# Attention and MLP block on one core: bias loaded by rows and turned on TensorE, first tiles of x from two queues, one tile's statistics on ScalarE

## The chip, the cores and the metric

The kernel runs on one NeuronCore of a Trainium2 chip. The metric is device time in microseconds (us); several executions were timed and the median stands for the kernel. One further execution was taken with the hardware profiler; its trace is read below.

The core's engines run side by side, each with a stream of instructions of its own, executed in order: TensorE (PE: matmuls, and transposes as matmuls with an identity), VectorE (DVE), ScalarE (ACT), GpSimd (POOL) and SyncE (SP), which here only issues DMAs. An engine that needs another's result waits on a semaphore, and whatever stands behind the waiting instruction on its engine waits too. SBUF is the on-chip memory (128 partitions), PSUM the accumulator that TensorE writes.

## The reference

x is 1 x 2048 x 512 in float32. A layer norm feeds attention with 32 query heads of 16 that share one key and value head; the normed x feeds both branches, x itself only the last sum:

```python
x = A_x
xn = _layernorm(x, axis=-1)              # (x - mean) / sqrt(var + 1e-5) over 512
s = _A_ref(xn, A_wq, A_wk, A_wv, A_wo)   # softmax(q k^T / 4) v, then @ wo
g = _silu(_B_ref(xn, B_w1, B_b1, B_w2))  # mish(xn @ w1 + b1) @ w2, 1792 wide
return x + s * g
```

So every product starts from the row statistics of x, and `b1` is added to the first MLP product, feature by feature.

## The kernel before

x is taken in 16 tiles of 128 rows, four to a block; block 0 is tiles 0 to 3. The program has a lead of some 75 us, in which the blocks are normed, turned and projected to keys and values and the first scores are made, and then a steady part, in which TensorE goes through scores, row maxima, value products and the MLP's products.

Numbers in float32 are multiplied as two parts: `hi` (rounded to the matmul format) and `lo` (the rest), so weights and x pass through a split (`split`, L460; for the key and value weights `wk_split`, L384) before a matmul reads them.

The start, by engine:

- **SP** issues the loads in the order in which the Python code calls them: `load_x(0)` (L381 calls L221 to L231: tiles 0 to 3 of x), the first query weights (`rawwq`, L514), then `load_x(1)`, in which tile 4 is followed by the two small loads `wkv` of the key and value weights (L229, L230), and further tiles, the first MLP weights, `b1` (L1292) and the other tiles.
- **POOL** clears some tiles (L195 to L199) and then runs `wk_split` (L384 to L389): four times a copy to the high part, a plain copy and a subtraction, twelve instructions on 128 x 64. They are recorded when `load_x(1)` is called, so they stand early in POOL's stream. Behind them stand the low parts of the first query weights (`wq`) and MLP weights (`xtw`).
- **DVE** takes the statistics of each tile (`stats`, L237: `bn_stats` and `bn_aggr` into `mvs`, mean and variance per row). After four tiles `norm_a` (L257) makes variance plus epsilon for the four at once (`ve`), ACT takes its power -1/2 with Ln and Exp (`norm_b`, L260), DVE refines it and makes `nbias` (`norm_c`, L264).
- Then `x_scale` (L284) norms the tiles, tiles 0 and 2 on DVE (L287) and 1 and 3 on ACT (L211); PE turns them (`x_transpose`, L293), ACT and DVE take them out as `xt` (L307, L169), and PE makes the first queries (`xps`, L112) and keys and values (`kp`, L339).
- For tiles 12 to 15 the statistics are on ACT (`stats_sum`, `stats_var`, L242 to L249), in two passes of 512 with accumulation.
- PE runs 24 matmuls on cleared data at the start (`warm`, L1299), and single ones later (L1384), whose results nobody reads.

The order inside each engine's stream in the lead comes from a small planner (L1286 to L1506): it holds tasks with guessed durations, dependencies and arrival times (`xat`), steps through its own clock, always takes the task that can start first, and records it there. It knows nothing of instructions that are recorded outside it, such as `wk_split`. A task is a Python function: if it has instructions for several engines, all are recorded at that moment.

`b1c` is `b1` as 14 columns of 128 partitions. It is loaded by one DMA in which each element is its own 4-byte piece, and its first reader is the bias addition at L785, in the MLP. `v_transpose` and `v_out` (L363, L374) turn the values of a block into `vaug`; for block 0 the copy out is on DVE.

Of the kernel before, what the change touches and what calls it, by code (L numbers as in the profile page):

```python
# [14 lines left out]
F32 = mybir.dt.float32  # L15
F32R = mybir.dt.float32r
AF = mybir.ActivationFunctionType
ALU = mybir.AluOpType
AX = mybir.AxisListType

P = 128
S = 2048
D = 512
# [7 lines left out]
NFT = F // P  # L31
# [91 lines left out]
def block_kernel(ctx: ExitStack, tc: tile.TileContext, x, wq, wk, wv, wo, w1, b1, w2, out):  # L123
    nc = tc.nc
    cp = ctx.enter_context(tc.tile_pool(name="const", bufs=1))
    sb = ctx.enter_context(tc.tile_pool(name="work", bufs=2))
    ps_e = ctx.enter_context(tc.tile_pool(name="ps_e", bufs=3, space=bass.MemoryType.PSUM))
    ps_m = ctx.enter_context(tc.tile_pool(name="ps_m", bufs=3, space=bass.MemoryType.PSUM))
    ps_v = ctx.enter_context(tc.tile_pool(name="ps_v", bufs=1, space=bass.MemoryType.PSUM))
# [4 lines left out]
    pe, act, dve, pool, sp = nc.tensor, nc.scalar, nc.vector, nc.gpsimd, nc.sync  # L134
# [51 lines left out]
    ident = cp.tile([P, P], F32, name="ident")  # L186
# [15 lines left out]
    b1c = cp.tile([P, NFT], F32, name="b1c")  # L202
# [4 lines left out]
    xr = x.rearrange("o (t p) d -> (o t) p d", p=P)  # L207
# [7 lines left out]
    def new_xt(c):  # L215
        xt_of[c] = sb.tile([P, 2, NDT, C], F32R, tag="xt", name=f"xt{c}", bufs=2)
        return xt_of[c]

    xin = {}

    def load_x(c):  # L221
        for tt in range(4):
            if 4 * c + tt < NPT:
                xin[c, tt] = pts[:, 4 * c + tt]
            else:
                xin[c, tt] = sb.tile([P, D], F32, tag=("y0", "sc")[tt % 2], name=f"xin{c}_{tt}", bufs=1)
            sp.dma_start(xin[c, tt], xr[4 * c + tt])
            if (c, tt) == (1, 0):
                sp.dma_start(wkv[:, 0], wk.rearrange("(t p) n -> p t n", p=P))  # L229
                sp.dma_start(wkv[:, 1], wv.rearrange("(t p) n -> p t n", p=P))  # L230
                wk_split()  # L231

    mvs = cp.tile([P, NKT, 2], F32, name="mvs")

    nms = cp.tile([P, 4], F32, name="nms")

    def stats(t):  # L237
        st = sb.tile([P, 6], F32, tag="st", name=f"st{t}")
        dve.bn_stats(st, xin[divmod(t, 4)])
        dve.bn_aggr(mvs[:, t], st)  # L240

    def stats_sum(t):  # L242
        w = sb.tile([P, D], F32, tag="u", name=f"sq{t}", bufs=2)
        act.activation(w, xin[divmod(t, 4)], AF.Identity, scale=-1.0 / 8192, accum_out=nms[:, t - 12:t - 11])

    def stats_var(t):
        w = sb.tile([P, D], F32, tag="t", name=f"sv{t}", bufs=2)
        act.activation(w, xin[divmod(t, 4)], AF.Square, scale=1.0 / 16, bias=nms[:, t - 12:t - 11],
                       accum_out=mvs[:, t, 1:2])  # L249
# [74 lines left out]
    vp_of = {}  # L324
# [38 lines left out]

    def v_transpose(c):
        if c == 0:
            vp = vp_of[c] = ps_v.tile([P, 4, 32], F32, tag="v", name=f"vp{c}")
            for tt in range(4):
                pe.transpose(vp[:, tt], vt_of[c][0:32, P * tt:P * (tt + 1)], ident[0:32, 0:32])
        else:
            vp = vp_of[c] = ps_v.tile([P, 2, 2, HALF], F32, tag="v", name=f"vp{c}")  # L370
            for j in range(2):
                pe.transpose(vp[:, j], vt_of[c][:, P * j:P * (j + 1)], ident)

    def v_out(c):  # L374
        if c == 0:
            dve.tensor_copy(vaug[:, 0:4, 0:DH], vp_of[c][:, :, 16:32])
        else:
            act.activation(vaug[:, 4 * c:4 * c + 4, 0:DH].rearrange("p (h j) n -> p h j n", h=2),
                           vp_of[c][:, :, :, 48:64].rearrange("p j h n -> p h j n"), AF.Copy)

    load_x(0)  # L381
    wkv = sb.tile([P, C], F32, tag="xr", name="wkv", bufs=4)
    wkv = wkv[:, 0:2 * NDT * DH].rearrange("p (a t n) -> p a t n", a=2, t=NDT)
    def wk_split():  # L384
        for j in range(4):
            o = slice(DH * j, DH * (j + 1))
            hi_pool(wk3[:, 0, :, o], wkv[:, j // 3])
            pool.tensor_copy(wkf[:, :, o], wkv[:, j // 3])
            sub(pool, wk3[:, 1, :, o], wkv[:, j // 3], f(wk3[:, 0, :, o]))  # L389
# [55 lines left out]
    def arrived(tag):  # L445
        k, n = todo[tag]
        if taken(tag, k) or tag == "ws" and k < 12 and k > posted[0] + (4 if lead and now[0] < 50 else 2):
            return False
        return k < n and items[tag][k].step + 1 <= (step[0] if lead else max(step[0], step_of(busy[0])) + 0.3)
# [45 lines left out]
    def load(tag):  # L495
        its = items[tag]
        k, n = todo[tag]
        if tag == "wx" and m1_done.get((NC - 2, NFT - 1)) is None or lead and tag == "wq" and n > 1:
            return
        if n == len(its):  # L500
            return
        it = its[n]
        if taken(tag, n) and (tag != "ws" or kept.get(it.key)):
            return
        if n == k and kept.get(it.key):
            it.tile = home(tag, n)
            sp.dma_start(f(it.tile), kept[it.key])
            it.ready = math.ceil(2 * (sp_at(0.5) + 1.6)) / 2
            todo[tag][:] = n + 1, n + 1
        elif n - k < NRAW[tag] and freed and freed[0] <= step[0] + (0.1 if lead else 0.8):  # L510
            freed.popleft()
            r = sb.tile([P, D], F32, tag="raw", name=f"raw{tag}{n}", bufs=RAWS)
            if len(it.src.shape) == 3:
                sp.dma_start(r.rearrange("p (t n) -> p t n", t=NDT), it.src)  # L514
            else:
                sp.dma_start(r, it.src)
            it.raw, it.step = r, (lead["arrive"]() if lead else sp_at(0.45))
            todo[tag][1] += 1
# [712 lines left out]
    plan = {e: [] for e in T}  # L1231
# [19 lines left out]
    def task(eng, us, fn, deps=(), **kw):  # L1251
        t = Task(eng, us, fn, deps, **kw)
        plan[eng].append(t)
        return t
# [28 lines left out]

    step[0] = (0.0 - E0) / STEP_US
    new_xt("w")
    xat = {0: 3.4, 1: 3.8, 2: 4.6, 3: 5.3}  # L1286
    dma_t[0], T["SP"] = 6.4, 2.0
    load("wq")
    load_x(1)
    xat.update({t: landed(DMA_US) for t in range(4, 8)})  # L1290
    load("ws")
    sp.dma_start(b1c, b1.rearrange("(t p) -> p t", p=P))  # L1292
    load_x(2)
    load_x(3)
    xat.update({t: landed(DMA_US) for t in range(8, 16)})
# [7 lines left out]
    def bank(tag, n, t, users):  # L1303
# [3 lines left out]
        b.append([t, *users])  # L1307

    st = [task("DVE", 0.83, lambda t=t: stats(t), at=xat[t], prio=t // 4 * 2) for t in range(12)]
    for t in range(12, 16):  # L1310
        ss = task("ACT", 0.8, lambda t=t: stats_sum(t), at=xat[t], prio=4)
        st.append(task("ACT", 0.8, lambda t=t: stats_var(t), [ss], prio=4))
    kv_done = None
    for c in range(NC):
# [56 lines left out]
        if c == 0:  # L1371
            vc.deps = [kl]
        bank("v", 1, k0, [kh, vc] if 0 < c < 3 else [kl, vc])
        vtr = task("PE", 0.5, lambda c=c: v_transpose(c), [vc], fill=c > 0)
        vo = task("ACT" if c else "DVE", 0.24, lambda c=c: v_out(c), [vtr])
        bank("v", 1, vtr, [vo])

# [42 lines left out]
    def soon(k, t):  # L1420

        return all(d.end is not None and d.end < t + 2.0 or d.end is None and d.deps and d.eng != "DVE" and all(x.end is not None for x in d.deps)
                   for d in k.deps)
# [4 lines left out]
    while True:  # L1428
# [59 lines left out]
        elif k == "J":  # L1488
            tag = next((g for g in ("wq", "ws", "wb") if not any(soon(k, s) for k in plan["POOL"]) and arrived(g) and busy[0] + E0 < s + (4.5 if g == "ws" else 0.5)), None)
            n = ran[0]  # L1490
# [193 lines left out]
```

## Time and profile before

| | |
|---|---|
| median of 3 executions | 1570.08 us (1569.93 to 1570.16) |
| the profiled execution | 1572.05 us |
| its span, first to last instruction | 1570.3 us |
| mean granted clock of TensorE in it | 0.997 |
| instructions in the span | 31407 |

The span is what the trace shows; the profiled execution's own time is 1.75 us longer, and 1.97 us longer than the median. The views used here are the page's share of busy time, the chain of waits that ended last (followed back from the last instruction to the first), the timeline of an engine, and the table of windows, which gives for chosen stretches the busy time of engines, the granted clock of TensorE, the busy share of the 16 DMA engines and the rate. A DVE or ACT instruction on a full tile of 128 x 512 float32 takes some 0.5 to 0.8 us here, so a few microseconds of the lead are a handful of instructions.

### The profile page before, as it was taken

What the parts mean: (1) busy time and instruction counts of PE and PEld (TensorE: products, weight loads), DVE (VectorE), ACT (ScalarE), POOL (GpSimd) and SP (SyncE); (2) the same over time, 40 slices, a digit from 0 to 9 for tenths busy, and PEclk for the clock granted to TensorE, in tenths of its full rate; (3) what the DMA queues carried; (4) which work ended last, traced back from release to release, by engine and by line L of the source; (5) the groups of instructions that cost most, each with busy time, mean ns of one, the idle gap of its engine ahead of it and who ended that gap; (6) DMA issues with size and microseconds to landing.
All of it is one profiled execution on the core that took longest, in us unless ns stands there. A gap on an engine that the chain in (4) does not pass through costs nothing.

```text
span 1570.3 us, 31407 instructions
## 1 busy us (share of the span) xinstructions
PE 1556.2 (99%) x11723; PEld 879.3 (56%) x11723; DVE 1348.8 (86%) x2281; ACT 1289.8 (82%) x2501; POOL 635.7 (40%) x668
## 2 busy tenths in 40 slices
PE   9999999999999999999999999999999999999998
PEld 5555655655555565565555556556555555655654
DVE  7998888888988988888998988888889998888844
ACT  5588888789898778977989788897788978888786
POOL 4687448356357202431624422163152323315022
PEclk9999999999999999999999999999999999999999
DMA  6233134133151303203113320322321213031110
GB/s 199 95 128 129 39 103 139 44 112 112 36 162 52 104 21 112 72 19 104 52 51 116 92 92 17 103 67 80 101 59 49 91 57 117 16 98 32 47 49 28
DMA packets 73863, 125.47 MB, mean 80 GB/s; under 512 B 21536, under 2 KB 35136, under 8 KB 73712
## 3 DMA queue, kind: packets, MB, share of 16 engines
q1 hardware_dynamic: 73568, 123.21, 25.3%
q8 instruction: 93, 1.52, 0.4%
q14 instruction: 58, 0.48, 0.1%
q10 hardware_dynamic: 144, 0.26, 0.0%
HBM read 75.57 MB, written 26.21 MB: 65 GB/s over the span
## 4 chain that ended last, share of the span: by engine, by line
PE 95%; ACT 2%; DVE 1%; DMA 1%; issue 0%; POOL 0%; SPq 0%; DVEq 0%; POOLq 0%; ACTq 0%
PE xps L116 43%; PE pv L1131 32%; PE m L1073 12%; PE e L1044 6%; PE xps L112 1%; ACT pts L1049 1%; DVE mb L1077 1%; PE kp L339 0%; DMA pts<-in_dram 0%; PE xp L298 0%; PE wop L116 0%; DMA rawwb<-in_dram 0%; PE warm L1384 0%; PE wop L112 0%; ACT xt L307 0%
## 5 line engine op out<-in xcount | busy, mean ns | idle before, releaser
L1077 DVE TENSOR_REDUCE mb<-m 128x1 f32<-128x512 f32 x2048 | 1266.8, 684 | 170.9 <-PE m L1073 145.4
L1049 ACT ACTIVATE pts<-e 128x512 f32<-128x512 f32 x2038 | 1060.1, 607 | 221.0 <-PE e L1044 152.3
L1073 PE MATMUL m<-ks,qt 48*128 48x512 f32 (+1 forms) x2048 | 842.5, 425 | 0.7 <-DVE mb L1077 0.5
L1044 PE MATMUL e<-qt,ks 64*128 64x512 f32 x2048 | 750.2, 407 | 2.1 <-ACT pts L1049 1.9
L1131 PE MATMUL pv<-pts,vaug 128*32 128x512 f32 x4076 | 530.1, 603 | 0.0
L1073 PEld LDWEIGHTS m<-ks,qt 48*128 48x128 f32 (+1 forms) x2048 | 368.1, 185 | 105.8 <-DVE mb L1077 53.4
L1044 PEld LDWEIGHTS e<-qt,ks 64*128 64x128 f32 x2048 | 373.9, 186 | 26.4 <-ACT pts L1049 12.6
L116 PE MATMUL xps<-wbs,act 64*128 64x512 f32 x1248 | 315.3, 397 | 0.0
L116 PE MATMUL xps<-xt,ws 64*128 64x512 f32 x1128 | 313.0, 410 | 0.4 <-ACT pts L1049 0.3
L116 PEld LDWEIGHTS xps<-xt,ws 64*128 64x128 f32 x1128 | 194.3, 185 | 183.0 <-ACT pts L1049 121.4
L116 PEld LDWEIGHTS xps<-wbs,act 64*128 64x128 f32 x1248 | 226.2, 185 | 65.3 <-ACT pts L1049 32.7
L1131 PEld LDWEIGHTS pv<-pts,vaug 128*32 128x32 f32 x4076 | 88.1, 108 | 151.4 <-issue 143.5
L169 POOL TENSOR_TENSOR hb<-hb,t 128x512 f32<-128x512 f32 x56 | 72.2, 1289 | 167.9 <-ACT t L804 87.7
L179 POOL TENSOR_SCALAR t<-t 128x512 f32<-128x512 f32 x56 | 34.4, 615 | 174.7 <-ACT t L791 174.6
L116 PE MATMUL xps<-xt,wq 64*128 64x512 f32 x336 | 93.1, 410 | 0.0
L116 PEld LDWEIGHTS xps<-xt,wq 64*128 64x128 f32 x336 | 57.9, 185 | 54.8 <-ACT pts L1049 37.7
L169 POOL TENSOR_TENSOR oc<-oc,sc 128x512 f32<-128x512 f32 (+1 forms) x16 | 20.7, 1291 | 153.7 <-DMA qt<-qh 78.6
L116 PE MATMUL xps<-wbs,ot_all 64*128 64x512 f32 x288 | 79.3, 408 | 0.0
L116 PEld LDWEIGHTS xps<-wbs,ot_all 64*128 64x128 f32 x288 | 49.5, 184 | 46.7 <-ACT pts L1049 28.5
L169 POOL TENSOR_TENSOR act<-hb,act 128x512 fp32r<-128x512 f32 x56 | 72.1, 1288 | 4.7
L169 POOL TENSOR_TENSOR hb<-hb,u 128x512 f32<-128x512 f32 x56 | 72.2, 1289 | 4.4
L169 POOL TENSOR_TENSOR u<-u,t 128x512 f32<-128x512 f32 x56 | 71.9, 1285 | 4.7
(154 smaller groups left out, 898.1 us busy)
## 6 DMA issues: line engine op xcount, KB each, us to landing
wbs<-w SPq DMA_DIRECT2D x38, 512.0 KB
ws<-w SPq DMA_DIRECT2D x36, 512.0 KB
qt<-qh SPq DMA_DIRECT2D x256, 32.0 KB
w<-wbs SPq DMA_DIRECT2D x14, 512.0 KB
wq<-wq SPq DMA_DIRECT2D x14, 512.0 KB
wbs<-wo SPq DMA_DIRECT2D x12, 512.0 KB
rawws<-in_dram SPq DMA_DIRECT2D x20, 256.0 KB
w<-ws SPq DMA_DIRECT2D x10, 512.0 KB
```

The source lines that it names most:

```text
L112: self.pe.matmul(ps, self.lhs(), self.rhs(), start=(self.k == 0), stop=(self.k == self.tot - 1))
L116: i = self.pe.matmul(ps, self.lhs()[o], self.rhs()[o], start=(self.k == 0 and self.halves == 0), stop=(self.k == self.tot - 1 and self.hal ...
L169: eng.tensor_tensor(out=o, in0=a, in1=b, op=op)
L179: pool.tensor_scalar(o, o, lim, 0.0, op0=ALU.min, op1=ALU.max)
L1044: pe.matmul(e, ks[o:o + 64, P * k:P * (k + 1)], q[o:o + 64, p], start=True, stop=True)
L1049: x = act.activation(dst, e, AF.Exp, scale=0.25)
L1073: pe.matmul(m, q[o, p, P * t:P * (t + 1)], ks[o, C * kb:C * (kb + 1)], start=True, stop=True)
L1077: return dve.reduce_max(out=mb_of[v][:, kb, z:z + 1], in_=m, axis=AX.X)
L1131: pe.matmul(o[32 * j:32 * j + 32], vaug[:, k], pt, start=(k == 0), stop=(k == 15))
```

## The change

Three things are done in one edit.

1. Tiles 1 and 3 of x are issued from ACT's queue, tiles 0 and 2 from SP's as before.
2. The statistics of tile 1 go from DVE (`stats(1)`) to a new task `stats_one` on ACT: a pass with Identity that sums -x/8192, a pass with Square around that sum, and then two POOL instructions that scale the sums into `mvs` for tile 1. DVE keeps tiles 0, 2 and 3.
3. `b1` is loaded as 14 rows of 128 (`b1r`), turned by one PE transpose into the PSUM tile in which block 0's values are turned, and copied to `b1c` by ACT.

```diff
--- before.py
+++ after.py
@@ -224,13 +224,14 @@
                 xin[c, tt] = pts[:, 4 * c + tt]
             else:
                 xin[c, tt] = sb.tile([P, D], F32, tag=("y0", "sc")[tt % 2], name=f"xin{c}_{tt}", bufs=1)
-            sp.dma_start(xin[c, tt], xr[4 * c + tt])
+            (act if c == 0 and tt % 2 else sp).dma_start(xin[c, tt], xr[4 * c + tt])
             if (c, tt) == (1, 0):
                 sp.dma_start(wkv[:, 0], wk.rearrange("(t p) n -> p t n", p=P))
                 sp.dma_start(wkv[:, 1], wv.rearrange("(t p) n -> p t n", p=P))
                 wk_split()
 
     mvs = cp.tile([P, NKT, 2], F32, name="mvs")
+    b1r = cp.tile([NFT, P], F32, name="b1r")
 
     nms = cp.tile([P, 4], F32, name="nms")
 
@@ -238,6 +239,16 @@
         st = sb.tile([P, 6], F32, tag="st", name=f"st{t}")
         dve.bn_stats(st, xin[divmod(t, 4)])
         dve.bn_aggr(mvs[:, t], st)
+
+    ms1 = cp.tile([P, 2], F32, name="ms1")
+
+    def stats_one():
+        x_ = xin[0, 1]
+        w = [sb.tile([P, D], F32, tag=g, name=f"s1{g}", bufs=2) for g in "ut"]
+        act.activation(w[0], x_, AF.Identity, scale=-1.0 / 8192, accum_out=ms1[:, 0:1])
+        act.activation(w[1], x_, AF.Square, scale=1.0 / 16, bias=ms1[:, 0:1], accum_out=ms1[:, 1:2])
+        pool.tensor_scalar(mvs[:, 1, 0:1], ms1[:, 0:1], -16.0, 0.0, op0=ALU.mult, op1=ALU.add)
+        pool.tensor_scalar(mvs[:, 1, 1:2], ms1[:, 1:2], 0.5, 0.0, op0=ALU.mult, op1=ALU.add)
 
     def stats_sum(t):
         w = sb.tile([P, D], F32, tag="u", name=f"sq{t}", bufs=2)
@@ -363,7 +374,10 @@
 
     def v_transpose(c):
         if c == 0:
-            vp = vp_of[c] = ps_v.tile([P, 4, 32], F32, tag="v", name=f"vp{c}")
+            v_b1 = ps_v.tile([P, P + NFT], F32, tag="v", name=f"vp{c}")
+            vp = vp_of[c] = v_b1[:, 0:P].rearrange("p (t n) -> p t n", n=32)
+            vp_of["b1"] = v_b1[:, P:P + NFT]
+            pe.transpose(vp_of["b1"], b1r, ident[0:NFT, 0:NFT])
             for tt in range(4):
                 pe.transpose(vp[:, tt], vt_of[c][0:32, P * tt:P * (tt + 1)], ident[0:32, 0:32])
         else:
@@ -374,6 +388,7 @@
     def v_out(c):
         if c == 0:
             dve.tensor_copy(vaug[:, 0:4, 0:DH], vp_of[c][:, :, 16:32])
+            act.activation(b1c, vp_of["b1"], AF.Copy)
         else:
             act.activation(vaug[:, 4 * c:4 * c + 4, 0:DH].rearrange("p (h j) n -> p h j n", h=2),
                            vp_of[c][:, :, :, 48:64].rearrange("p j h n -> p h j n"), AF.Copy)
@@ -1283,13 +1298,13 @@
 
     step[0] = (0.0 - E0) / STEP_US
     new_xt("w")
-    xat = {0: 3.4, 1: 3.8, 2: 4.6, 3: 5.3}
+    xat = {0: 4.3, 1: 4.3, 2: 4.6, 3: 5.3}
     dma_t[0], T["SP"] = 6.4, 2.0
     load("wq")
     load_x(1)
     xat.update({t: landed(DMA_US) for t in range(4, 8)})
     load("ws")
-    sp.dma_start(b1c, b1.rearrange("(t p) -> p t", p=P))
+    sp.dma_start(b1r, b1.rearrange("(t p) -> t p", p=P))
     load_x(2)
     load_x(3)
     xat.update({t: landed(DMA_US) for t in range(8, 16)})
@@ -1307,6 +1322,8 @@
         b.append([t, *users])
 
     st = [task("DVE", 0.83, lambda t=t: stats(t), at=xat[t], prio=t // 4 * 2) for t in range(12)]
+    plan["DVE"].remove(st[1])
+    st[1] = task("ACT", 1.7, stats_one, at=xat[1], lat=0.5)
     for t in range(12, 16):
         ss = task("ACT", 0.8, lambda t=t: stats_sum(t), at=xat[t], prio=4)
         st.append(task("ACT", 0.8, lambda t=t: stats_var(t), [ss], prio=4))
```

What stands now in each engine's stream, where it matters. On POOL, at the end of `wk_split` (`wk` and `wkf` are its outputs, `mvs` the statistics, `wq` and `xtw` the low parts of weights). Before:

```order
L164 TENSOR_SCALAR wk_90<-wkv 128x4x16 [waits DMAHW7_49]
L388 COPY wkf<-wkv 128x4x16
L169 TENSOR_TENSOR wk_90<-wkv,wk_90 128x4x16 [waits Pool_49]
L169 TENSOR_TENSOR wq_193<-rawwq_115,wq_193 128x512 [waits DMAHW4_49,Activation_49]
L169 TENSOR_TENSOR xtw<-rawws_135,xtw 128x512 [waits DMAHW3_49,Activation_49]
```

and now (line numbers are those of the changed file):

```order
L164 TENSOR_SCALAR wk_90<-wkv 128x4x16 [waits DMAHW7_49]
L403 COPY wkf<-wkv 128x4x16
L169 TENSOR_TENSOR wk_90<-wkv,wk_90 128x4x16 [waits Pool_49]
L250 TENSOR_SCALAR mvs<-ms_107 128x1 [waits Activation_49]
L251 TENSOR_SCALAR mvs<-ms_107 128x1 [waits Activation_49]
L169 TENSOR_TENSOR wq_198<-rawwq_117,wq_198 128x512 [waits DMAHW4_49,Activation_49]
L169 TENSOR_TENSOR xtw<-rawws_137,xtw 128x512 [waits DMAHW3_49,Activation_49]
```

The two instructions that finish tile 1's statistics came in behind all twelve instructions of `wk_split`.

On DVE, from the statistics to `ve` (`norm_a`). Before:

```order
L239 BN_STATS st_180<-pts 128x6 [waits DMAHW2_49]
L240 BN_AGGR mvs<-st_180 128x2 [waits DVE_49]
L239 BN_STATS st_183<-pts 128x6 [waits DMAHW3_49]
L240 BN_AGGR mvs<-st_183 128x2 [waits DVE_49]
L258 TENSOR_SCALAR ve<-mvs 128x4 [waits DVE_49]
```

and now:

```order
L240 BN_STATS st_185<-pts 128x6 [waits DMAHW3_49]
L241 BN_AGGR mvs<-st_185 128x2 [waits DVE_49]
L240 BN_STATS st_188<-pts 128x6 [waits DMAHW2_49]
L241 BN_AGGR mvs<-st_188 128x2 [waits DVE_49]
L269 TENSOR_SCALAR ve<-mvs 128x4 [waits DVE_49,Pool_49]
```

`ve` of block 0 waited for DVE alone and now waits for POOL as well.

On ACT, after the power for block 2 (`rstd`), where the bias is copied out (`vp` is the shared PSUM tile, `sq` and `sv` the statistics of tile 12, `xf` the turned tile 7). Before:

```order
L262 ACTIVATE rstd<-rstd 128x4 [waits Activation_49]
L244 ACTIVATE sq_373,nms<-pts 128x512 [waits DMAHW1_49]
L248 ACTIVATE sv_390,mvs<-pts,nms 128x512 [waits Activation_49]
L316 ACTIVATE xf_0_329<-xp_385 128x2x128 [waits PE_49]
L316 ACTIVATE xf_1_330<-xp_385 128x2x128
```

and now:

```order
L273 ACTIVATE rstd<-rstd 128x4 [waits Activation_49]
L391 ACTIVATE b1c<-vp_362 128x14 [waits DVE_49,PE_49]
L255 ACTIVATE sq_380,nms<-pts 128x512 [waits DMAHW1_49]
L259 ACTIVATE sv_397,mvs<-pts,nms 128x512 [waits Activation_49]
L327 ACTIVATE xf_0_334<-xp_392 128x2x128 [waits PE_49]
L327 ACTIVATE xf_1_335<-xp_392 128x2x128
```

The copy of the bias came in ahead of the statistics, with a wait for DVE: the DVE instruction that it waits for is the copy of block 0's values out of the same PSUM tile. Beside these rows only the matching ones changed: two DMA issues and two activations at the head of ACT's stream, one pair of statistics gone from DVE's, one transpose more on PE. All other instructions stand in the order in which they stood.

## The prediction

> **What bounds the kernel now.** The page's busy shares come first:
>
> ```profile
> PE 1556.2 (99%) x11723; PEld 879.3 (56%) x11723; DVE 1348.8 (86%) x2281; ACT 1289.8 (82%) x2501; POOL 635.7 (40%) x668
> ```
>
> TensorE works all the time, and none of its real work is touched. What the change can move is how late the steady part begins, so the start of the chain of waits is next (start, length, what):
>
> ```profile
> 1.64 4.70 DMA pts<-in_dram
> ...
> 7.89 0.19 DVE mvs L240
> ...
> 8.11 0.18 DVE ve L258
> ...
> 9.62 1.53 ACT pts L211 x2
> ...
> 11.17 2.07 ACT xt L307 x4
> ...
> 13.29 3.20 PE xps L112 x12
> ...
> 16.51 0.60 ACT qh L723
> 17.11 0.12 ACT rstd L261
> ...
> 19.32 0.78 POOL pts L287
> ...
> 20.14 0.66 PE xp L298 x4
> ```
>
> The reader is to see that `ve` at 8.11 us is the neck: norming, turning, first queries, block 1's norm follow from it one after the other, and in each engine's stream all other work stands behind it. Only loads and POOL's `wk_split` run without it. What makes `ve` late by some time makes the lead late by as much; I see no slack behind it, since what is loaded later waits for buffers that this chain frees.
>
> **Part 1: POOL.** The timeline of POOL (start, length, engine, line, what):
>
> ```profile
> 3.46 1.84 POOL L199 MEMSET qt<- 128x1024 f32 x2
> 9.33 0.24 POOL L164 TENSOR_SCALAR wk<-wkv 128x64 fp32r<-128x64 f32 x1 [4.03 <-DMA wkv<-in_dram]
> ...
> 10.01 0.42 POOL L164 TENSOR_SCALAR wk<-wkv 128x64 fp32r<-128x64 f32 x1
> ...
> 11.13 0.23 POOL L164 TENSOR_SCALAR wk<-wkv 128x64 fp32r<-128x64 f32 x1
> ...
> 12.46 1.29 POOL L169 TENSOR_TENSOR wq<-rawwq,wq 128x512 fp32r<-128x512 f32 x1
> ...
> 18.18 0.20 POOL L275 TENSOR_SCALAR hv<-hv 128x4 f32<-128x4 f32 x1
> 18.45 0.20 POOL L276 TENSOR_TENSOR rstd<-hv,rstd 128x4 f32<-128x4 f32 x1
> ```
>
> POOL is idle for 4.03 us until `wkv` lands at 9.33, then splits until 12.46, and the two instructions that finish tile 1's statistics stand behind that. `ve` waits for them. Before, `ve` was done before the split began. Three of the four rounds of the split take 0.67 us (9.33 to 10.01, and two from 11.13 to 12.46) and one, in which DVE normed tiles, 1.12 (10.01 to 11.13). In the changed kernel DVE stands still meanwhile, so I take 4 x 0.67 = 2.7 us; at most it is the 3.13 of before. The two small instructions cost one step of 0.27 and 0.20 (18.18, 18.45), and 0.05 for the semaphore.
>
> When does `wkv` land? SP's queue issues tiles 0 to 3 in
>
> ```profile
> 0.74 1.81 SPq L227 DMA_DIRECT2D pts<-in_dram  x4
> ```
>
> and the windows show how busy the DMA engines then are (length, busy us and count of PE, PEld, DVE, ACT, POOL, then clock, DMA share, GB/s):
>
> ```profile
> 2.00:3.00 1.00, 1.00 (x2) 0.81 (x3) 0.00 (x0) 0.01 (x1) 1.00 (x2) 1.00 0.80 287
> 3.00:4.00 1.00, 1.00 (x4) 0.80 (x3) 0.53 (x1) 0.00 (x0) 1.00 (x3) 1.00 0.89 307
> 4.00:5.00 1.00, 1.00 (x4) 0.81 (x3) 0.93 (x4) 0.00 (x0) 1.00 (x2) 1.00 0.88 250
> ```
>
> The same bytes stand ahead of `wkv` as before. Two issues of 0.45 us leave SP's queue, but the DMA engines are 80 to 89% busy from 2 us on, so there is 0.20 + 0.11 + 0.12 = 0.4 us to win. I take 0.2, between 0 and 0.5. [...]
>
> So `ve` starts at 9.33 - 0.2 + 2.7 + 0.52 = 12.35, which is **4.2 us late**; bounds 9.33 - 0.5 + 2.7 + 0.52 - 8.11 = 3.9 and 9.33 + 3.13 + 0.52 - 8.11 = 4.9. I take 4.3, because POOL's low part of `wq`, which ran after DVE's norming, now falls into it, and that norming may lose some tenths (the round of 1.12 shows that the two disturb each other).
>
> The gains of the change are hidden by this: DVE has one tile less to take and tiles may land sooner, but DVE then waits for POOL until 12.3. ACT's two passes cost what those of tile 12 cost:
>
> ```profile
> 23.85 0.61 ACT L244 ACTIVATE sq<-pts 128x512 f32<-128x512 f32 x1
> ...
> 25.22 0.19 ACT L248 ACTIVATION_READ_ACCUMULATOR sv<-pts,nms 128x1 f32 x1
> 25.24 0.22 DVE L376 COPY vaug<-vp 128x64 f32<-128x64 f32 x1
> ...
> 25.58 0.66 ACT L316 ACTIVATE xf<-xp 128x256 f32<-128x256 f32 x2 [0.17 <-PE xp L298]
> ...
> 28.53 1.98 PE L339 MATMUL kp<-xf,wkf 128*64 128x256 f32 x8
> ```
>
> 25.22 + 0.19 - 23.85 = 1.6 us, from about 4 to 6 us, before POOL can use them. Cost nothing; without the split ahead on POOL they would end before tile 3's statistics.
>
> **Part 2: the bias.** The load by rows replaces one of 4-byte pieces in SP's queue; nobody waited for that. The transpose adds at most the 0.16 us of one of four in `20.14 0.66`, in a stretch where PE waits for loads. ACT's copy waits for DVE's copy of `vaug`, which stands behind four maxima on DVE. In the times of before that holds ACT from 23.9 to 25.46; behind it are the statistics of tile 12 (1.6 us) and `xf`, which would be done at 25.5 + 0.25 + 1.6 + 0.66 = 28.0 instead of 26.24. The reader of that `xf` is `kp` at 28.53. So it is hidden with 0.5 us to spare: 0, at most 0.5.
>
> **Part 3: TensorE's clock.** PE's timeline ahead of the first queries:
>
> ```profile
> 9.03 0.61 PE L1384 MATMUL warm<-qt 128*128 128x512 f32 x2
> 10.38 1.97 PE L298 MATMUL xp<-ident,pts 128*128 128x128 f32 x16 [0.73 <-DVE pts L287]
> ```
>
> Between the end of the warm-up, 9.64, and the first transpose, which moves from 10.38 to 14.7, PE has 5 us without work. What an idle stretch does is shown at the end of the trace (only PE was asked for; clock after the count):
>
> ```profile
> 1.98:5.12 3.14, 3.14 (x7) 1.00 0.85 281
> 5.12:8.53 3.41, 3.41 (x16) 1.00 1.12 303
> ...
> 22.19:25.60 3.41, 3.17 (x15) 1.00 0.31 74
> 25.60:29.02 3.42, 3.42 (x12) 0.50 0.23 49
> ...
> 32.43:35.85 3.42, 3.42 (x20) 1.00 0.41 116
> ...
> 1565.01:1568.42 3.41, 0.62 (x3) 1.00 0.74 275
> 1568.42:1570.30 1.88, 0.00 (x0) 0.50 0.16 59
> ```
>
> A stretch of 3.41 us with 0.62 us of work is followed by half the clock. The clock falls and rises at 25.60 and 32.43, two such stretches apart. On the grid that these edges give, counted back in steps of 3.41, the stretch from 11.95 to 15.36 would hold 0.6 us of work, so the clock falls at 15.36. The warm-up has the price: 7 matmuls in 3.14 us (0.45 each; the view has no clock record there) against 16 in 3.41 (0.21). For transposes:
>
> ```profile
> 25.11 0.44 PE xp L298 x4
> ...
> 27.74 0.85 PE xp L298 x4
> 28.60 1.91 PE kp L339 x8
> ...
> 32.80 0.58 PE kp L339 x4
> ```
>
> 0.85 instead of 0.44 us for a tile. Four tiles then take 3.4 - 0.3 us (the first begins at full speed) from 14.7 to 17.9, where ACT paces them at 0.5 each before; the three warm matmuls behind them take 1.35; the queries begin at 19.2 instead of 13.29 + 4.3 = 17.6. That is 1.5 us. If the clock returns at 18.77 the total is about 1.4; if at 22.19, seven of twelve queries run at half speed and the end is at 23.5 instead of 20.8: 2.7. I take **2.1**, between 0 and 2.9. All of it is on the path, since `qh` at 16.51 holds ACT's `rstd` of block 1. [...]
>
> The half-speed stretch that the kernel has anyway, 25.60 to 32.43, costs some 2.4 us (1.91 for eight `kp` against 2 x 0.58 = 1.16 is 0.75 of it, the rest like it over 6.8 us). It could vanish or grow when the work moves on the grid. The whole shift, 6.4, is nearly two stretches of 3.41, so I leave it as it is: 0, bounds -2.4 and +1.
>
> **Sum.** 4.3 + 2.1 = 6.4 us. The profiled execution's 1572.05 becomes 1578.45; it lies 1.97 above the median of the runs, so the median becomes **1576.5**.
>
> **Rivals.** First, the wait without the clock: the clock holds, or what it costs is won back in the later stretch. Then 1570.1 + 4.3 = 1574.4 (1573.4 to 1575.3). For it: the stretch from 8.53 to 11.95 keeps a microsecond of warm-up, and a grid that lies otherwise leaves less idle in any one stretch. Against: 5 us are longer than one stretch.
>
> Second, the lead takes the delay up: DVE waits long for PE between block 1 and block 3, and its maxima could run closer. Then only a part arrives, some 2 us: 1572. Against: all those maxima follow from the same `ve`, and the order is the same.
>
> Third, not slower: `wkv` lands while POOL is still clearing, by 5.3 us (3.46 + 1.84), the split is through before tile 3's statistics, and POOL's two instructions cost nothing. Then `ve` is early by what the loads win, 0.4: 1569.7. It decides at a landing by about 5 us; the trace has 9.33, and the bytes ahead did not change.
>
> **How the numbers follow.** Forecast 0.58; first rival 0.25; second 0.07; third 0.05; later than 1578.5 (both half-speed stretches longer, ACT's wait not hidden) 0.05. Low end: first rival's 1573.4. High end: 4.9 + 2.9 + 0.6 = 8.4 gives 1578.5. Outside are 0.17. A change under 0.2% (3.1 us) can't be told from none: slower 0.58 + 0.25 + 0.05 = 0.88, same 0.10, faster 0.02, for a `wkv` so early that the later half-speed stretch vanishes as well.
>
> **What would show it.** In the timeline of POOL, the two `mvs` instructions start right behind the last `wk`, near 12; DVE's `ve` waits for POOL and starts at 12.0 to 13.0; ACT's passes end by 6.5. The windows show clock 0.50 somewhere between 12 and 22, and the first queries start near 19 and end near 23. The first transposes of block 1 (20.14 before) start at 26 to 27. I am wrong if `ve` starts before 11, if the clock stays at 1.00 until 22, or if scores at 90 us stand less late than the transposes of block 1.

## The result, and the profile after

| | before | after |
|---|---|---|
| median of 6 executions each, side by side | 1570.12 us | 1577.09 us |
| lowest and highest | 1569.93 to 1573.25 | 1576.28 to 1577.48 |
| the profiled execution, its span, its mean clock | 1572.05, 1570.3, 0.997 | 1576.44, 1574.6, 0.997 |

The changed kernel takes 1.0037 times as long, 95% interval 1.0026 to 1.0048: 7.0 us more, where 6.4 were predicted (1576.5). The profiled execution of after is one of the shorter of the six, 6.3 us over the median of before; what the median has beyond it, 0.65, is in no trace. One thing has to be known to read the two profiles: the stretch at half clock from 25.60 to 32.43, which the profile of before shows, comes in about one execution of that kernel in three, as far as the mean clocks of the executions tell, and is not in the profile of after.

The page's busy shares (busy us, share, number of instructions) of after:

```profile
PE 1557.2 (99%) x11724; PEld 879.1 (56%) x11724; DVE 1349.3 (86%) x2279; ACT 1291.5 (82%) x2506; POOL 635.6 (40%) x670
```

No engine works more than it did by over 1.7 us, so time went into waiting. The chain of waits (start, length, what) shows where; the last engine before `ve` is POOL now:

```profile
2.67 5.40 DMA wkv<-in_dram
...
10.95 0.19 POOL mvs L250
...
11.22 0.20 POOL mvs L251
...
11.44 0.18 DVE ve L269
...
12.71 1.27 DVE nbias L266
14.01 0.56 DVE pts L298
...
14.61 3.67 PE xp L309 x16
18.28 1.29 PE warm L1401 x3
...
19.71 3.14 PE xps L112 x12
...
22.88 0.60 ACT qh L738
```

Set against the rows of before, `ve` is 3.33 us late (8.11 to 11.44). `nbias`, a 128x4 instruction, stands in the chain of before as

```profile
9.38 0.21 DVE nbias L255
```

and takes 1.27 now, and the norming is 4.39 late (9.62 to 14.01). The sixteen transposes take 3.67 instead of the 1.97 of before's timeline, the first queries are 6.42 late (13.29 to 19.71), and `qh` is 6.37 late.

The timeline of POOL in after (start, length, engine, line, operation, tiles; in brackets the idle time ahead and what ended it) shows the first `wk` of the split, the last, the two instructions on `mvs` right behind it, and then the low part of `wq`:

```profile
8.15 0.24 POOL L164 TENSOR_SCALAR wk<-wkv 128x64 fp32r<-128x64 f32 x1 [2.85 <-DMA wkv<-in_dram]
...
10.55 0.32 POOL L169 TENSOR_TENSOR wk<-wkv,wk 128x64 fp32r<-128x64 f32 x1
10.95 0.19 POOL L250 TENSOR_SCALAR mvs<-ms 128x1 f32<-128x1 f32 x1
11.22 0.19 POOL L251 TENSOR_SCALAR mvs<-ms 128x1 f32<-128x1 f32 x1
12.69 1.26 POOL L169 TENSOR_TENSOR wq<-rawwq,wq 128x512 fp32r<-128x512 f32 x1 [1.28 <-ACT wq L482]
```

DVE's timeline shows the wait for POOL, and that `nbias` (12.71 + 1.26 = 13.97) ends with POOL's `wq` (12.69 + 1.26 = 13.95):

```profile
11.44 0.17 DVE L269 TENSOR_SCALAR ve<-mvs 128x4 f32<-128x4 f32 x1 [3.89 <-POOL mvs L251]
...
12.71 1.26 DVE L266 SCALAR_TENSOR_TENSOR nbias<-mvs,rstd 128x4 f32<-128x4 f32 x1
```

In the windows (stretch; length, busy us and count of PE, clock, DMA share, GB/s) the clock is half from about 13.07 to 19.90, behind a stretch in which PE had half a microsecond of work, and whole again later:

```profile
9.65:13.07 3.42, 0.51 (x3) 1.00 1.01 349
13.07:16.48 3.41, 1.87 (x9) 0.50 1.01 374
16.48:19.90 3.42, 3.27 (x13) 0.50 0.07 25
...
25.60:29.02 3.42, 2.76 (x18) 1.00 0.22 54
29.02:32.43 3.41, 3.35 (x17) 1.00 0.28 70
```

### The profile page after: what moved, and what is told of

It reads as the page before. It is cut to its first block, busy times and chain, and to the rows that moved or that the text cites. A ratio compares the mean times of both kernels' runs of the same rounds, so it can differ in the third digit from the quotient of the medians.

```text
span 1574.6 us, 31414 instructions
## 1 busy us (share of the span) xinstructions
PE 1557.2 (99%) x11724; PEld 879.1 (56%) x11724; DVE 1349.3 (86%) x2279; ACT 1291.5 (82%) x2506; POOL 635.6 (40%) x670
## 4 chain that ended last, share of the span: by engine, by line
PE 96%; ACT 2%; DVE 1%; DMA 0%; POOL 0%; issue 0%; SPq 0%; ACTq 0%; POOLq 0%
PE xps L116 42%; PE pv L1146 32%; PE m L1088 12%; PE e L1059 7%; PE xps L112 1%; ACT pts L1064 1%; PE xp L309 1%; DVE mb L1092 1%; PE kp L350 0%; DMA wkv<-in_dram 0%; PE warm L1401 0%; PE wop L116 0%; PE wop L112 0%; ACT hb L800 0%; DVE xr L169 0%
```

## The experiments

The theory: the two POOL instructions stand behind `wk_split`, which waits for `wkv`; that makes `ve` late, and the idle TensorE then loses half its clock. The rivals: only one of the two; the two queues or the bias; and, once the profile of after was read, POOL's `wq` beside `nbias`. For the first four kernels the kernel before ran on the same chip with a median of 1569.93 us (30 executions).

**1. The split behind the two instructions.** The changed kernel, with `wk_split` recorded after them and the planner's charges kept where they were:

```diff
             if (c, tt) == (1, 0):
...
-                wk_split()
+                for _ in range(4):
+                    charge(0.7)
+                    charge(1.3)
...
         pool.tensor_scalar(mvs[:, 1, 1:2], ms1[:, 1:2], 0.5, 0.0, op0=ALU.mult, op1=ALU.add)
+        b = busy[0]
+        wk_split()
+        busy[0] = b
```

> The changed kernel with one thing moved: the twelve instructions of wk_split are recorded behind the two POOL instructions that finish tile 1's statistics, not ahead of them. All other streams stand as in the change. Theory (place in POOL's stream): the whole loss comes from that place. Then the two instructions run at about 6.4 us, ve starts at 7.6 to 7.9 instead of 11.4, PE has no idle stretch of 5 us, the clock is 1.00 until the first queries are through, and the time is 1569.3 to 1570.5, 6.5 to 7.7 below the change. Rival (the new loading from two queues, ACT's statistics or the bias cost time by themselves): the time stays above 1572.

Measured: 1569.96 us (11 executions), 0.9999 of before (0.9990 to 1.0007). Its POOL timeline:

```profile
5.38 0.19 POOL L252 TENSOR_SCALAR mvs<-ms 128x1 f32<-128x1 f32 x1
6.03 0.19 POOL L253 TENSOR_SCALAR mvs<-ms 128x1 f32<-128x1 f32 x1 [0.46 <-ACT s1t L251]
8.23 0.24 POOL L164 TENSOR_SCALAR wk<-wkv 128x64 fp32r<-128x64 f32 x1 [2.00 <-DMA wkv<-in_dram]
```

and its chain:

```profile
13.41 3.19 PE xps L112 x12
...
16.62 0.60 ACT qh L743
```

The two instructions end at 6.2, before tile 3's statistics; queries and `qh` stand within 0.12 us of before. All three parts of the change are in this kernel, so the whole loss hangs on the place of two small instructions in POOL's stream. `ve` comes at 7.69 here instead of 8.11 (at 7.78 with the two queues alone, experiment 3), and nothing of that is seen in the time. PE's timeline has a reason: the transposes begin at 10.66, straight behind the warm-up matmuls, where before they began at 10.38 after 0.73 of waiting for DVE. In experiments 3, 4 and 7 too they stand straight behind the warm-up. So a late `ve` holds the lead, and an early one is held up by the warm-up.

**2. The warm-up longer.** The changed kernel with 42 warm-up matmuls, so that TensorE is busy until the transposes come:

```diff
-NWARM = 24
+NWARM = 42
```

> The changed kernel with 42 instead of 24 warm-up matmuls at the start, so that TensorE's idle stretch from 10.1 to 14.6 us is nearly filled; ve stays late. Theory (late start plus clock): ve is at 11.4 as in the change, the clock stays 1.00 through the first queries, which end near 21 instead of 22.9, and the time falls by 1.5 to 2.5, to 1574.6 to 1575.6. Rival (the clock costs nothing on the path, the late start alone makes the difference, or it is given back later): 1576.5 to 1577.6, unchanged.

Measured: 1574.30 us (8 executions), 1.0025 (1.0015 to 1.0036). Its chain:

```profile
13.93 1.52 ACT pts L211 x2
15.48 2.07 ACT xt L318 x4
17.59 3.20 PE xps L112 x12
20.82 0.60 ACT qh L738
```

The norming starts as in after (13.93 against 14.01), but `qh` stands at 20.82 instead of 22.88: the half clock cost 2.0 us there. The profiled executions differ by 1576.44 - 1574.31 = 2.1. The rest of the loss, `qh` at 20.82 against 16.51, is not the clock's. In the medians this kernel lies 4.4 us over its before and the change 7.0 over its own, 2.6 between them, a little more than the 1.5 to 2.5 expected. The median is not to be leant on as closely; the kernel was run again (experiment 10).

**3 and 4. One part alone: two queues, or the bias.** The kernel before with the changed line of `load_x` only; and with only `b1r`, its load, transpose and copy, all as in the diff of the change.

> The kernel before with one part of the change alone: tiles 1 and 3 of x issued from ACT's queue. Theory: the loads are not what costs time; ve starts between 7.4 and 8.1, time 1569.3 to 1570.6. Rival (two queues share the DMA engines, so that the first tile comes later and the four tiles' statistics end later): ve after 8.5 and a time above 1571.

> The kernel before with one part of the change alone: the bias by rows, turned by PE with block 0's values and copied by ACT. Theory: ACT's copy waits 1.5 us for DVE's copy of the values, but kp of block 1 hides it; time 1569.9 to 1570.7. Rival (that wait reaches kp of block 1 and the maxima behind it): 1571.5 or more.

Measured: two queues 1569.76 us, 0.9996 (0.9988 to 1.0005); the bias 1569.23 us, 0.9991 (0.9982 to 0.9999), 11 executions each. Neither loses. In the bias kernel ACT's copy does wait, in its timeline

```profile
23.30 0.21 ACT L263 ACTIVATE rstd<-rstd 128x4 f32<-128x4 f32 x1
24.87 0.18 ACT L381 ACTIVATE b1c<-vp 128x14 f32<-128x14 f32 x1 [1.36 <-PE xp L299]
```

for 1.36 us, though the row names PE: the copy of `vaug` on DVE ends just ahead of it,

```profile
24.56 0.21 DVE L380 COPY vaug<-vp 128x64 f32<-128x64 f32 x1
```

But in PE's timeline the keys of block 1 follow the maxima matmuls by 26.79 - 24.79 = 2.00 us:

```profile
24.79 1.13 PE L1078 MATMUL m<-ks,qt 64*128 64x512 f32 x3
...
26.79 1.12 PE L340 MATMUL kp<-xf,wkf 128*64 128x256 f32 x8
```

just as in the kernel with two queues, which has no such wait:

```profile
25.51 1.13 PE L1073 MATMUL m<-ks,qt 64*128 64x512 f32 x3
...
27.51 1.08 PE L339 MATMUL kp<-xf,wkf 128*64 128x256 f32 x8
```

So the wait costs nothing. The bias kernel came out below the 1569.9 to 1570.7 expected, and its interval ends just under 1, but in its profiled execution tiles landed early (`ve` at 7.46, ahead of anything that the bias touches), and experiment 7 did not repeat it; a gain of its own is not shown.

**5. POOL's low part of `wq` in pieces.** The kernel of experiment 2 with the 128x512 subtraction on POOL as four of 128 columns:

```diff
-        sub(pool, w[:, 1], it.raw, f(w[:, 0]))
+        if it.key == ("q", 0) and lead:
+            charge(1.3)
+            for z in range(0, D, P):
+                pool.tensor_tensor(out=w[:, 1, z:z + P], in0=it.raw[:, z:z + P], in1=f(w[:, 0, z:z + P]), op=ALU.subtract)
+        else:
+            sub(pool, w[:, 1], it.raw, f(w[:, 0]))
```

> The changed kernel with the longer warm-up of 42 matmuls (to hold the clock still) and with POOL's low part of the first query weights made in four instructions of 128 columns instead of one of 512. In the changed kernel DVE's nbias took 1.26 us instead of 0.20, ending as POOL's instruction of 1.26 us ended. Theory (DVE is held until the POOL instruction that runs beside it ends): nbias then takes 0.2 to 0.5, the norming starts 0.7 to 1.0 earlier, and the time is 1573.2 to 1573.8 against 1574.3 with the longer warm-up alone. Rival (the 1.26 us has another cause, or it ran beside POOL by chance): nbias stays above 1 us, 1574.0 to 1574.6.

Measured: 1574.99 us (1573.42 to 1576.80, 11 executions), 1.0026 (1.0017 to 1.0034). POOL's timeline has the four pieces in one row, and in DVE's timeline `nbias` shrinks with the piece it meets:

```profile
12.94 2.09 POOL L488 TENSOR_TENSOR wq<-rawwq,wq 128x128 fp32r<-128x128 f32 x4 [1.29 <-ACT wq L482]
...
12.96 0.46 DVE L266 SCALAR_TENSOR_TENSOR nbias<-mvs,rstd 128x4 f32<-128x4 f32 x1
```

From `ve` to the norming it is 13.45 - 11.69 = 1.76 us, against 13.93 - 11.33 = 2.60 with one piece. The mechanism came as expected. In the profiled executions the time followed: `qh` stands at 20.39 instead of 20.82, and the time is 1573.86 instead of 1574.31 us. It did not follow in the median, which lies over the expected 1573.2 to 1573.8, and this experiment alone leaves open why.

**6 and 7. The statistics alone, and the other two parts together.** The kernel before with `stats_one`, its task and the changed `xat`; and the kernel before with the queues and the bias.

> The kernel before with one part of the change alone: tile 1's statistics on ACT with the two finishing instructions on POOL; loads and bias as before. Theory (ve waits for wkv to land, plus the split): the loss is there in full without the other two parts, and since wkv lands later from one queue (8.7 to 9.3 instead of 8.1), ve is at 11.9 to 12.7 and the time 0.4 to 1.2 above the change, 1577.3 to 1578.3. Rival (the loss needs the loads from ACT's queue): below 1573.

> The kernel before with the two parts of the change that lost nothing by themselves: two queues and the bias by rows; statistics as before. Theory: both act off the path that sets the end, ve at 7.5 to 7.9, time 1569.0 to 1570.2, not told from before. Rival (the 0.7 us by which the bias alone lay under before is a gain of its own and adds to the queues'): 1568.9 or less.

Measured: the statistics alone 1577.35 us (5 executions), 1.0040 (1.0027 to 1.0053), all of the loss (0.3 above the change, where 0.4 to 1.2 were expected); the other two 1569.63 us (11 executions), 0.9994 (0.9985 to 1.0003), not to be told from before. The chain of the statistics kernel, in which all tiles come from SP's queue, also prices the second queue:

```profile
3.62 5.29 DMA wkv<-in_dram
...
12.29 0.18 DVE ve L268
```

The load of `wkv` that the split waits for (L229 in SP's queue) is issued 0.95 us later than in after (3.62 against 2.67), and takes as long (5.29 against 5.40). The time to landing varies, though: in before and in experiment 4 the load is issued at 3.61 and 3.62 as well, and the split starts at 9.33 and 8.66.

**8. `nbias` ahead of POOL's `wq`.** In after and in experiments 2 and 6, POOL's `wq` starts 0.02 to 0.03 us ahead of `nbias`. The kernel of experiment 2, with a copy on ACT and an instruction on POOL that only hold POOL back by some 0.3 us:

```diff
             act.activation(w[:, 0], it.raw, AF.Copy)
+            if it.key == ("q", 0):
+                act.activation(late[:, 0:1], two, AF.Copy)
+                pool.tensor_scalar(late[:, 1:2], late[:, 0:1], 0.5, 0.0, op0=ALU.mult, op1=ALU.add)
```

> Longer warm-up kernel with POOL's first low part of wq held back by some 0.3 us: a 128x1 copy on ACT behind the high part of wq, and a 128x1 instruction on POOL that reads it, both of no use, stand ahead of it. In the longer warm-up kernel POOL's wq started at 12.58 and DVE's nbias at 12.60, and nbias ended with POOL's instruction, 1.29 us later. Theory (whoever starts first holds the other for its whole instruction): nbias is first now and takes 0.16 to 0.20; from ve to the norming 1.5 to 1.6 instead of 2.60, first queries about 16.5 instead of 17.59, qh about 19.7 instead of 20.82, and the time 0.8 to 1.2 below 1574.3, about 1573.3; POOL's low part itself may end later by some tenths. Rival (two engines that share a path slow each other whichever starts first): nbias takes 0.5 or more again, norming starts at most 0.3 earlier. Second rival (the time does not follow the lead at this size, as in the kernel with the pieces): nbias 0.2 and qh 19.7, but the time stays at 1574 to 1575.

Measured: 1574.19 us (11 executions), 1.0021 (1.0012 to 1.0030). The expectation failed in its sum. DVE's timeline:

```profile
12.74 0.16 DVE L267 SCALAR_TENSOR_TENSOR nbias<-mvs,rstd 128x4 f32<-128x4 f32 x1
12.94 2.04 DVE L299 TENSOR_SCALAR pts<-pts,rstd,nbias 128x512 f32<-128x512 f32 x2
```

`nbias` is short, but now the two norming instructions take 2.04 instead of 1.00 (in the chain the first has 1.60 of it, from 12.94), while POOL's `wq` runs undisturbed:

```profile
12.96 1.28 POOL L169 TENSOR_TENSOR wq<-rawwq,wq 128x512 fp32r<-128x512 f32 x1
```

DVE's norming stood first in the records, by 0.02, and was held all the same. So a lead of that size in the records does not tell who holds whom, and the hold had only moved on by one instruction.

**9 and 10. POOL's `wq` behind the norming, beside experiment 2 again.** Six such instructions in a row instead of one; and the kernel of experiment 2, unchanged, on the same chip (before there: 1570.82 us, 18 executions).

```diff
-                pool.tensor_scalar(late[:, 1:2], late[:, 0:1], 0.5, 0.0, op0=ALU.mult, op1=ALU.add)
+                for z in range(6):
+                    pool.tensor_scalar(late[:, 1 - z % 2:2 - z % 2], late[:, z % 2:z % 2 + 1], 0.5, 0.0, op0=ALU.mult, op1=ALU.add)
```

> As the kernel before it (nbias ahead), but six 128x1 instructions of no use on POOL instead of one, each on the result of the last, so that the low part of wq starts some 1.6 us behind ACT's high part, near 14.4, when DVE's two norming instructions are through. In the kernel with one of them nbias fell to 0.16, but the two norming instructions took 2.04 instead of 1.00, and queries began at 17.40 instead of 17.59. Theory (DVE's instructions of this kind can't run while POOL's low part runs, wherever they meet): nbias 0.2, the norming pair 1.0 to 1.2, first queries 16.3 to 16.7, qh 19.5 to 19.9, time 0.8 to 1.2 below the longer warm-up kernel of the same call. Rival (the pair took 2.04 for a reason of its own, say it waits for ACT or its tile): it takes 2.0 again and the queries begin at 17.2 or later. Second rival (lead and time part): queries at 16.5, time the same as the longer warm-up kernel.

> The longer warm-up kernel unchanged, as the one to compare the kernel with six POOL instructions with on the same chip: nbias 1.26 to 1.29 again, POOL's low part of wq starting at most 0.05 ahead of it, queries at 17.4 to 18.0 by when wkv lands, 1.0020 to 1.0030 of before. If nbias comes first by chance in this execution and takes 0.2, then the order of the two is not fixed by the program and the norming pair takes 2.0 instead.

Measured: 1574.42 us (1573.68 to 1575.96, 11 executions), 1.0019 (1.0011 to 1.0028), and 1576.64 us (1574.21 to 1577.59, 8 executions), 1.0030 (1.0019 to 1.0041). With `wq` at 14.89 neither `nbias` nor the norming is held, as DVE's timeline shows:

```profile
11.60 0.17 DVE L270 TENSOR_SCALAR ve<-mvs 128x4 f32<-128x4 f32 x1 [3.97 <-POOL mvs L252]
...
12.87 0.16 DVE L267 SCALAR_TENSOR_TENSOR nbias<-mvs,rstd 128x4 f32<-128x4 f32 x1
13.06 1.00 DVE L299 TENSOR_SCALAR pts<-pts,rstd,nbias 128x512 f32<-128x512 f32 x2
```

and PE's timelines have the first queries, here

```profile
16.73 3.19 PE L112 MATMUL xps<-xt,wq 128*128 128x512 f32 x12 [0.40 <-ACT xt L319]
```

5.13 us behind `ve`; before had 13.29 - 8.11 = 5.18, and the kernel beside it, with `ve` at 11.27,

```profile
17.53 2.71 PE L112 MATMUL xps<-xt,wq 128*128 128x512 f32 x10 [0.39 <-ACT xt L318]
```

6.26. The meeting of POOL's `wq` with DVE costs 1.1 us of lead, and this kernel gets it back; in `qh` 0.8 of it is seen (19.95 against 20.75), since `ve` came 0.33 later. The medians differ by 2.2, where 0.8 to 1.2 were expected, and the profiled times, 1575.96 and 1577.51, by 1.55. Both profiles have a stretch of half clock later in the lead; the windows of experiment 10 show it as

```profile
25.00:28.50 3.50, 3.13 (x20) 1.00 0.26 66
28.50:32.00 3.50, 3.31 (x9) 0.60 0.21 52
32.00:35.50 3.50, 3.50 (x14) 0.50 0.64 246
```

The clock fell inside the second of these windows, at about 29.2. By the mean clocks, that stretch also accounts for the two medians of one kernel, 1574.30 and 1576.64. Of its 16 executions the six with a mean clock of 1.000, and two with 0.999, took 1574.0 to 1574.4 us; three more with 0.999 took 1575.7 to 1575.9, and the five with 0.998 took 1577.3 to 1577.6. A median says how often the stretch came as well as what the edit is worth. The lowest executions point the same way as the profiles, but they are single ones: 1574.02 and 1574.21 for this kernel, 1573.42 with the pieces, 1573.68 with `wq` behind the norming. Seven of the eleven with the pieces took 1574.6 to 1576.8 at clocks of 0.998 to 1.000, and why is left open, as is what any of these edits is worth in the median below about 1 us.

## Why the prediction was right, point by point

**What bounds the kernel: right for a late `ve`.** Its delay, with what followed, passed through queries (6.42), `qh` (6.37) and block 1's first transposes (20.14 to 26.49, 6.35), and experiment 1 took all of it away at once. The twelve profiles show that it arrives whole: in the nine without a half-clock stretch behind `qh`, the profiled execution's time less the start of `qh` is 1552.9 to 1554.0 us, while `qh` itself stands anywhere from 16.06 to 23.97. For an early `ve` the warm-up is the neck instead (experiment 1).

**Part 1, POOL: the right wait, with two terms off that cancel.** The two `mvs` instructions stand right behind the split and DVE waits for them, as said. The split took 8.15 to 10.87, 2.72 (2.7 taken); from its end to `ve` it is 0.57 (0.52 taken). But `wkv` landed for a split at 8.15 rather than 9.33 - 0.2 = 9.13, so `ve` came at 11.44 and not 12.35. The step that failed is "there is 0.20 + 0.11 + 0.12 = 0.4 us to win": it took the busy DMA engines as the limit, while experiment 6 and after have the same 5.3 to 5.4 us from issue to landing, issued 0.95 earlier. Over all profiles with two queues the split starts at 7.97 to 8.37, with one queue at 8.66 to 9.33. What was saved is about the two issues of 0.45 that left SP's queue, 0.9 in all.

The other term is "that norming may lose some tenths", put at 0.1. The low part of `wq` met `nbias` and cost 1.1. `nbias` took 0.16 to 0.21 where it did not meet the low part, 1.26 to 1.29 beside one POOL instruction of 1.26 to 1.29, and 0.46 beside pieces (2.09 for four, 0.52 each): each time it ended within 0.04 of the instruction or piece that it met, so it was held to the end and not slowed in proportion. What holds it is not shown.

So the norming is 4.39 late by 3.33 + 1.06, where 4.3 stood in the sum. That the total fits is luck: -0.9 and +1.0 cancel.

**Part 2, the bias: right.** ACT waits and it costs nothing (experiment 4). **Statistics on ACT: right.** The passes end at 6.34, and without the split ahead POOL is through before DVE (experiment 1).

**Part 3, the clock: right in size, early in time.** From `ve` to the first queries after takes 8.27; take off 5.18 as before and 1.08 for the meeting with POOL, and 2.0 are left, the same as in `qh` against experiment 2, where 2.1 was taken. The fall came at 13.07 and not at 15.36 (at about 14.45 in experiment 6): the edges counted from before's records in steps of 3.41, the author's estimate, do not hold for another execution. All sixteen transposes so ran at half the clock (3.67 instead of 1.97), but the clock was back at 19.90, for the queries. The 2.1 was picked between 1.4 and 2.7, which were worked out for the other edges (and the 1.5 on the way to them is 19.2 - 17.6 = 1.6), so that the size fits this closely is in part luck.

**The later stretch: the step that was wrong.** "I leave it as it is: 0, bounds -2.4 and +1" took a chance event for a part of the kernel. Of 30 executions of before, ten took 1571.5 to 1573.2 us, nine of them with a mean clock of 0.997 or 0.998; the other twenty, with 0.999 or 1.000, took 1569.0 to 1570.9. The profiled execution, with 0.997, was of the first kind, which accounts for the 1.97 by which it lay above the median. By subtracting them the sum came out for executions without the stretch, so the end figure was spared. The size, some 2.4, was about right: in the three profiles with the stretch (before, experiments 9 and 10) the time less the start of `qh` is 1555.5 to 1556.8, some 2 to 3 us more than in the other nine. The test that "scores at 90 us stand less late than the transposes of block 1" did come true, and would have called the theory wrong: the first score matmul in PE's timelines, before and after, is

```profile
82.89 0.38 PE L1044 MATMUL e<-qt,ks 64*128 64x512 f32 x1
...
86.43 0.39 PE L1059 MATMUL e<-qt,ks 64*128 64x512 f32 x1
```

only 3.54 late. Against profiles without any half clock, 80.55 in experiment 1 and 80.41 in experiment 3, it is 5.9 to 6.0 late, near the 6.35.

**The rivals.** The wait without the clock is not what happened in after, but experiment 2 made it: at full clock it takes 1574.0 to 1574.4, where 1574.4 was worked out, though from other terms (`ve` 3.2 late there and 1.1 lost at `nbias`). The lead does not take the delay up. Nor did `wkv` land early enough: 8.15 is far from "about 5".

In the queries the account is 3.33 for `ve`, 1.08 for the meeting with POOL and 2.0 for the clock, 6.4 in all.

## What to carry to other kernels

Moving a small piece of work to an engine that looks idle cost here what stood ahead of it in that engine's stream (3.33 us at `ve`): look for the first instruction there that waits for a transfer, and record the small ones ahead of it. When a short instruction suddenly takes as long as another engine's long one (here 1.26 beside 1.26, instead of 0.21), look whether both end together. And before a stretch at half clock is counted as part of a kernel, look at several executions: here the profile of before had one that two executions in three do not have.

## What was not expected of the hardware

- DVE's instructions of 0.16 us (`nbias`, 128x4) or 0.5 us (the norming, 128x512) took 1.26 to 1.29 and 1.60 beside the low part of `wq`, a POOL instruction of 1.26 to 1.29 us, the second also where DVE's record starts 0.02 us ahead (experiment 8).
- TensorE's clock fell to half for some 7 us in the lead of several executions (25.60 to 32.43 in before, 13.07 to 19.90 in after, from about 29.2 in experiment 10). In after the fall came behind 0.51 us of work in 3.42. In before it came behind 3.17 us of work in 3.41 (22.19 to 25.60) while none followed on 2.71 in the 3.42 just ahead (18.77 to 22.19), and in experiment 10 it came behind 3.13 in 3.50 (25.00 to 28.50), at least by the busy time of the records. What decides there is not shown.
- With loads issued from two engines, the split started 0.8 us earlier on average (8.17 over nine profiles against 8.99 over three), although the DMA engines had been 80 to 89% busy (before, 2 to 5 us).
